# One of four first-layer bias operations moves to GpSimd, and every other group one more to VectorE

## The chip, the cores and the metric

The kernel runs on one core of a Trainium2 chip. A core has TensorE (PE in the profile; PEld is its weight load), VectorE (DVE), ScalarE (ACT), GpSimd (POOL) and SyncE (SP), which work side by side, each through its own instructions in order, and 16 DMA engines. Times are device microseconds (us). The kernel before took 1106.79 us, the median of three runs (1106.64 to 1107.31).

## What is computed

An attention layer with a learned position bias, followed by two gated layers. The part that the change touches is the bias: for every query position and key position a hidden layer of 32 units is made from one number, and a second layer turns it into one bias for each of 8 heads.

```python
scores = scale * np.matmul(q, k.transpose(0, 1, 3, 2))       # 4 batches, 8 heads, 576 positions
psi_rel = np.log1p(np.abs(pos[:, None] - pos[None, :]))
psi_i = np.log1p(np.maximum(pos[:, None], 1.0))
x = (psi_rel / psi_i)[..., None]
h = np.maximum(x @ w1 + b1, 0.0)                              # first layer, 32 hidden units
bias = h @ w2                                                # second layer, 8 heads
scores = scores + bias.transpose(2, 0, 1)[None]
attn = softmax(scores);  x = attn @ v
x = (sigmoid(x @ w_gate) * (x @ w_val)) @ w_out
h = x @ w_in;  out = (h * clip(h + 3, 0, 6) / 6) @ w_out2
```

## The kernel before

The 576 query positions are cut into five chunks: four of 128 and one of 64. For each chunk the kernel makes the bias, then the attention of 32 batch and head pairs (as 16 units of two heads), and then the two gated layers, which are cut into 68 steps. The gated layers of a chunk run together with the bias and the attention of the next chunk in one "block". Only the first chunk's bias and attention stand alone, at the start. That start is called the lead here.

**The bias of a group.** A group is 16 query positions. 32 hidden units times 4 positions fill 128 partitions, so a group takes four first-layer operations, g = 0 to 3, each on 128x576 numbers: `bias_hidden(G, g, act)` at L136. Operations with g below `act` (2, if nothing is said) are done by ScalarE at L147 as relu(x * scale + b1), the others by VectorE at L149 as max(x * scale, -b1). The second form lacks the addition of b1. What is missing is the same for all keys, w2 times b1, and is put back later through the bias column `cv_t` (L120), whose rows 64 to 127 belong to g = 2 and 3. The result of a group is the tile `z`, of 18,432 bytes a partition, from the pool `z_p` of two buffers (L72), which lives for the whole kernel.

TensorE multiplies z with w2, eight products a group (`bias_mm`, L170), each g into its own 32 rows of a PSUM tile. There are two such PSUM tiles. VectorE then writes the group's bias to the tile `bo` (`bias_out`, L227), SyncE copies the first two heads of it to the mask `bm` of the first attention units (L233), and after every second group GpSimd's queue issues the transfer of the pair to `biasD` in memory (L235). For later chunks the bias depends on the distance alone in a simpler way ("mirrored", L162, L195, L201, L190).

**The order.** In the lead the order of the instructions on TensorE, ScalarE, VectorE and SyncE is that of the code (L648). GpSimd's order is left to the planner, which puts the instructions in the order in which it expects them to become ready. Groups 0 to 7 are the first chunk, 8 to 11 the beginning of the second. In the loop at L657 group G's four first-layer operations and products come first, then the output of group G - 1; the output of group 7 comes ahead of group 8. After the loop come the scores of the first unit (`att_qk`, L309), groups 10 and 11 with `act` = 1, and then the loop over the 16 units: exponentials (L334), row factors, transposes (L360) into the tile `pT`, sums with v (`att_av`, L404), and a split of the result into two parts, `xyh` (ScalarE, L424) and `xyl` (VectorE, L425), which the gated layers read.

In the blocks only TensorE and SyncE are in the order of the code; the planner orders VectorE and ScalarE. Groups 12 to 15 belong to the first block, but their z needs nothing of the lead but a free z buffer.

**Memory.** The lead has its own tiles, in pools that are stacked in the order of L646: `pt` (two of 4,608 bytes a partition), `s` (three of 4,608), `k`, `v`, `bo`, `wf`, `cv`. When the lead ends, the pools made by `late` (L705) take the same memory from the beginning on: `bo` first (4,864 bytes), then the tiles of the gated layers. An operation on a late tile waits for the tiles of the lead that lay there.

Of the kernel before, what the change touches and what calls it, by code (L numbers as in the profile page):

```python
# [9 lines left out]
F32 = mybir.dt.float32  # L10
# [9 lines left out]
NI = 288  # L20
# [38 lines left out]
def fused_kernel(ctx: ExitStack, tc: tile.TileContext, qd, kd, vd, tz, td, rd, zc, w2b, iden, wpack, out):  # L59
# [11 lines left out]
    bm_p = pool("bm", 2)  # L71
    z_p = pool("z", 2)  # L72
    w_p = pool("w", 6)
# [20 lines left out]
    zc_t = const.tile([128, 3], F32, name="zc_t")  # L94
    cv_t = const.tile([128, 1], F32, name="cv_t")
    wm_t = const.tile([128, 1], F32, name="wm_t")
    w2b_t = const.tile([128, 32], F32, name="w2b_t")
# [7 lines left out]
    nc.vector.memset(id_t, 0.0)  # L105
    nc.vector.memset(cv_t, 0.0)
    ps = mm_ps()
    for _ in range(9):
# [5 lines left out]
    ps = mm_ps()  # L114
    for g in (2, 3):
        nc.tensor.matmul(
            out=ps[32 * g:32 * g + 32, 0:2], lhsT=w2b_t, rhs=zc_t[:, 0:2], start=True, stop=True,
            tile_position=(0, 32 * g),
        )
    nc.vector.tensor_scalar(out=cv_t[64:128], in0=ps[64:128, 1:2], scalar1=D ** 0.5, scalar2=None, op0=ALU.mult)  # L120

# [14 lines left out]
    def bias_hidden(G, g, act=2):  # L136

        if g == 0:
            z_q[G] = z_p.tile([128, 4, S], F32, name="z")
        t = 4 * G + g  # L140
        if mirrored(G):
            n = reach(G)[2]
            z, x = z_q[G][:, g, 0:n], td_t[:, 0:n]
        else:
            z, x = z_q[G][:, g], tz_t[:, S - 4 - 4 * t:2 * S - 4 - 4 * t]
        if g < act:
            nc.scalar.activation(out=z, in_=x, func=AF.Relu, scale=sc_t[:, t:t + 1], bias=b1c)  # L147
        else:
            nc.vector.tensor_scalar(  # L149
                out=z, in0=x, scalar1=sc_t[:, t:t + 1], scalar2=zc_t[:, 2:3], op0=ALU.mult, op1=ALU.max  # L150
            )
# [25 lines left out]
    def bias_out2(G, apart=False):  # L177
# [6 lines left out]
        if apart:  # L184
            for x, p in enumerate((ps, bo_q.pop(G + 1))):
                nc.scalar.activation(
                    out=bo[:, x, left:SU], in_=p[:, 0:right + 1], func=AF.Identity, scale=D ** 0.5, bias=cv_t
                )
            for x, p in enumerate((ps, p)):
                nc.vector.tensor_scalar(  # L190
                    out=bo[:, x, 0:left], in0=p[:, left:0:-1],
                    scalar1=D ** 0.5, scalar2=cv_t, op0=ALU.mult, op1=ALU.add,
                )
        else:
            nc.scalar.activation(  # L195
                out=bo[:, :, left:SU], in_=ps[:, :, 0:right + 1], func=AF.Identity, scale=D ** 0.5, bias=cv_t
            )
# [18 lines left out]
    def bias_out(G, x=0, last=True):  # L216
# [7 lines left out]
        if c:  # L224
            nc.scalar.activation(out=bv, in_=ps[:, :, 0:NI], func=AF.Identity, scale=D ** 0.5, bias=cv_t)
        else:
            nc.vector.tensor_scalar(  # L227
                out=bv, in0=ps[:, :, 0:NI], scalar1=D ** 0.5, scalar2=cv_t, op0=ALU.mult, op1=ALU.add
            )
# [415 lines left out]
    with ExitStack() as lead:  # L645
        for name, bufs in (("pt", 2), ("s", 3), ("k", 6), ("v", 7), ("bo", 3), ("wf", 2), ("cv", 2)):  # L646
            A[name] = lead.enter_context(tc.tile_pool(name=name + "l", bufs=bufs))
# [9 lines left out]
        for G in range(NG0 + NG1 + 1):  # L657
            if G == NG0:
                bias_out(G - 1, (G - 1) % 2, G % 2 == 0)
            if G < NG0 + NG1:  # L660
                for g in range(4):
                    bias_hidden(G, g)
                bias_mm(G)
# [43 lines left out]

    A["bo"] = late("bo", 1)
    P = dict(gu=late("gu", 12), tmp=late("tmp", 3), acc=late("acc", 4))
    A.update(k=late("k", 4), v=late("v", 4), s=late("s", 2))  # L710
# [213 lines left out]
```

## Time and profile before

| what | value |
|---|---|
| median of three runs | 1106.79 us |
| time of the profiled execution | 1106.79 us |
| its span, first to last instruction | 1105.0 us |
| TensorE busy | 1094.5 us |
| VectorE busy | 668.0 us |
| ScalarE busy | 524.7 us |
| GpSimd busy | 129.7 us |
| first chunk's bias, first z to last output | 4.75 to 20.05 us |
| attention of the first chunk | 24 to 88 us |

In the rows below a time in front is the start in us from the span's start, the second number is how long the instruction or the merged run of instructions lasted; "x2" is their count, and square brackets give the idle time of the engine just before and what ended it. Instructions of one engine can overlap a little: the next begins while the one before drains. A busy TensorE in the rows is not a TensorE at its peak, since matmuls are pipelined and their ends are modelled.

### The profile page before, as it was taken

How to read it: one execution, taken by the hardware profiler on the slowest of the kernel's cores; microseconds unless marked ns; L12 is line 12 of the kernel's file. 1: busy time of each engine (PE TensorE's matmuls, PEld its weight loads, DVE VectorE, ACT ScalarE, POOL GpSimd, SP SyncE). 2: the span in 40 equal slices, each digit the busy share in tenths (PEclk: the TensorE clock that was granted, in tenths of full speed). 3: DMA queues.
4: the chain of work that ended last, by engine and by line, in shares of the span. 5: the costliest groups of instructions: out<-in, count | busy, mean ns of one | idle time of the engine just before them, and what ended most of it. 6: DMA issues, size and time to landing. Idle time of an engine off the chain costs nothing.

```text
span 1105.0 us, 19878 instructions
## 1 busy us (share of the span) xinstructions
PE 1094.5 (99%) x7142; PEld 884.0 (80%) x7142; DVE 668.0 (60%) x1529; ACT 524.7 (47%) x1052; POOL 129.7 (12%) x248
## 2 busy tenths in 40 slices
PE   8999999999999999999999999999999999999998
PEld 4777777777777788777888878788788787879998
DVE  7999998898963456897725654656252417052232
ACT  7887686798863433565414342534032214121132
POOL 1000000000010002112221111111430202031000
PEclk9999999999999999999999999999999999999999
DMA  6958999999987688999988888798896978778997
GB/s 228 369 182 296 373 396 373 386 322 375 384 292 233 219 264 281 283 311 294 342 296 249 292 245 278 250 281 244 283 274 239 266 247 255 227 215 310 363 365 270
DMA packets 118769, 321.97 MB, mean 291 GB/s; under 512 B 21008, under 2 KB 29712, under 8 KB 118672
## 3 DMA queue, kind: packets, MB, share of 16 engines
q1 hardware_dynamic: 108000, 297.15, 79.0%
q0 software_dynamic: 9152, 23.21, 7.5%
q8 instruction: 57, 0.93, 0.3%
q10 hardware_dynamic: 1520, 0.35, 0.1%
q14 instruction: 40, 0.33, 0.1%
HBM read 245.09 MB, written 51.37 MB: 268 GB/s over the span
## 4 chain that ended last, share of the span: by engine, by line
PE 80%; DVE 7%; DMA 5%; ACT 4%; issue 3%; POOL 1%; ACTq 0%; DVEq 0%; POOLq 0%
PE ps L574 63%; PE ps L404 7%; PE ps L309 3%; PE ps L446 3%; PE ps L360 2%; DMA pT<-t 2%; PE ps L162 1%; PE ps L170 1%; DVE cm L546 1%; DMA wsp<-wp 1%; DVE cm L549 1%; DVE wp L555 1%; POOL outT L635 1%; ACT cm L544 1%; DVE s L324 1%
## 5 line engine op out<-in xcount | busy, mean ns | idle before, releaser
L574 PE MATMUL ps<-xyh,wp 128*128 128x512 f32 (+1 forms) x1600 | 468.1, 372 | 0.3
L574 PEld LDWEIGHTS ps<-xyh,wp 128*128 128x128 f32 x1600 | 290.5, 189 | 61.3 <-issue 4.9
L574 PE MATMUL ps<-gh,wp 128*128 128x512 f32 (+1 forms) x1120 | 330.2, 373 | 0.0
L574 PE MATMUL ps<-xyl,wp 128*128 128x512 f32 (+1 forms) x800 | 295.6, 370 | 0.4 <-DVE xyl L587 0.3
L574 PEld LDWEIGHTS ps<-gh,wp 128*128 128x128 f32 x1120 | 203.5, 189 | 37.8 <-issue 3.6
L574 PE MATMUL ps<-gl,wp 128*128 128x512 f32 (+1 forms) x560 | 206.9, 369 | 0.0
L574 PEld LDWEIGHTS ps<-xyl,wp 128*128 128x128 f32 x800 | 151.1, 189 | 24.6 <-DVE xyl L587 0.8
L383 POOL DMA_DIRECT2D pT<-t x192 | 94.3, 499 | 504.1 <-DVE t L373 136.3
L583 ACT ACTIVATE gh<-tmp 128x512 fp32r<-128x512 f32 (+1 forms) x140 | 82.2, 588 | 145.9 <-DVE tmp L605 103.3
L334 ACT ACTIVATE s<-s,m 128x576 f32<-128x576 f32 x144 | 110.4, 768 | 20.1 <-DVE m L468 14.4
L574 PEld LDWEIGHTS ps<-gl,wp 128*128 128x128 f32 x560 | 105.8, 189 | 16.8 <-DVE gl L585 0.6
L585 DVE TENSOR_TENSOR gl<-tmp,gh 128x512 fp32r<-128x512 f32 (+1 forms) x140 | 88.6, 634 | 47.3 <-ACT gh L583 46.4
L605 DVE SCALAR_TENSOR_TENSOR tmp<-tmp,ps 128x512 f32<-128x512 f32 (+1 forms) x60 | 37.8, 630 | 94.1 <-PE ps L574 92.7
L404 PEld LDWEIGHTS ps<-pT,vt 128*64 128x64 f32 x1600 | 79.4, 137 | 18.1 <-issue 12.6
L404 PE MATMUL ps<-pT,vt 128*64 128x128 f32 (+1 forms) x1600 | 92.4, 266 | 1.5 <-DMA pT<-t 0.9
L611 DVE SCALAR_TENSOR_TENSOR tmp<-tmp,ps 128x512 f32<-128x512 f32 (+1 forms) x80 | 50.0, 628 | 57.1 <-ACT tmp L610 55.5
L424 ACT ACTIVATE xyh<-ps 128x128 fp32r<-128x128 f32 (+1 forms) x52 | 16.5, 317 | 107.3 <-PE ps L404 107.1
L610 ACT ACTIVATE tmp<-ps 128x512 f32<-128x512 f32 (+1 forms) x80 | 43.9, 549 | 41.9 <-PE ps L574 40.4
L425 DVE TENSOR_TENSOR xyl<-ps,xyh 128x128 fp32r<-128x128 f32 (+1 forms) x52 | 17.7, 341 | 72.4 <-ACT xyh L424 72.1
L601 ACT ACTIVATE tmp<-ps 128x512 f32<-128x512 f32 (+1 forms) x60 | 33.1, 552 | 56.9 <-PE ps L574 56.9
L635 POOL DMA_DIRECT2D outT<-acc x40 | 27.7, 736 | 262.3 <-DVE acc L626 245.1
L147 ACT ACTIVATE z<-tz_t,zc_t,sc_t 128x576 f32<-128x576 f32 (+7 forms) x70 | 49.7, 766 | 13.2 <-PE ps L162 11.3
(73 smaller groups left out, 1096.5 us busy)
## 6 DMA issues: line engine op xcount, KB each, us to landing
wp<-wsp SPq DMA_DIRECT2D x272, 512.0 KB, 5.2
wd<-wpack SPq DMA_DIRECT2D x68, 512.0 KB, 6.7
wsp<-wp SPq DMA_DIRECT2D x68, 512.0 KB, 6.2
vt<-vd SPq DMA_DIRECT2D x80, 320.0 KB, 5.2
kt<-kd SPq DMA_DIRECT2D x80, 288.0 KB, 5.1
pT<-t POOLq DMA_DIRECT2D x192, 72.0 KB, 5.3
pT<-t SPq DMA_DIRECT2D x128, 72.0 KB, 5.0
bm<-biasD SPq DMA_DIRECT2D x15, 576.0 KB, 5.9
```

Of the source, the lines that this page charges most:

```text
L147: nc.scalar.activation(out=z, in_=x, func=AF.Relu, scale=sc_t[:, t:t + 1], bias=b1c)
L309: nc.tensor.matmul(out=ps[h][n * a:n * a + n, j, 0:NI], lhsT=qt[r, b + a, 0:n], rhs=kt[r, NI * j:NI * j + NI], start=True, stop=True, tile ...
L334: nc.scalar.activation(out=s[:, h], in_=s[:, h], func=AF.Exp, scale=-1.0, bias=d["m"][:, h:h + 1], accum_out=r[:, h:h + 1],)
L383: (nc.sync if p[0][0] < 4 and i > 1 else nc.gpsimd).dma_start(out=pt[32 * q:32 * q + 32, i].rearrange("j u t i -> j (u t i)"), in_=t[32 * ...
L404: nc.tensor.matmul(out=po[64 * h:64 * h + 64, n * a:n * a + n], lhsT=vt[:, v], rhs=pt[:, m * a:m * a + m, k, :], start=(t == 0), stop=(t = ...
L574: nc.tensor.matmul(out=ps[:, 0:nt], lhsT=w[:, c, :], rhs=x[:, 0:nt], start=(first and c == 0 and i == 0), stop=(last and c == 3 and i == 2),)
L583: nc.scalar.activation(out=hi[:, 0:nt], in_=src, func=AF.Copy, scale=scale)
L585: nc.vector.tensor_tensor(out=lo[:, 0:nt], in0=src, in1=hi[:, 0:nt].bitcast(F32), op=ALU.subtract)
L605: nc.vector.scalar_tensor_tensor(out=th, in0=th, scalar=1.0, in1=ps, op0=ALU.add, op1=ALU.mult)
L610: nc.scalar.activation(out=t, in_=ps, func=AF.Relu, bias=3.0)
L611: nc.vector.scalar_tensor_tensor(out=t, in0=t, scalar=6.0, in1=ps, op0=ALU.min, op1=ALU.mult)
L635: q.dma_start(out=out[2 * ih + x, o, :, :, lo - ih * NI:hi - ih * NI], in_=av[:, 2 * x:2 * x + 2, lo - i0:hi - i0],)
```

## The change

Of a first-chunk group's four first-layer operations GpSimd makes the last (g = 3). ScalarE makes the first two in even groups and the first alone in odd ones, and VectorE the rest: one in even groups, two in odd ones. The columns that put w2 times b1 back follow: `cv_t` for groups with two ScalarE operations, the new `cv1_t` for those with one, which is also used for groups 10 and 11. The z tiles come from a pool of three buffers that belongs to the lead, and from a pool of two late buffers after it, which lies behind the late `bo`. The persistent pool is gone.

```diff
-    z_p = pool("z", 2)
...
+    cv1_t = const.tile([128, 1], F32, name="cv1_t")
...
+    nc.vector.memset(cv1_t, 0.0)
...
-    for g in (2, 3):
+    for g in (1, 2, 3):
         nc.tensor.matmul(
             out=ps[32 * g:32 * g + 32, 0:2], lhsT=w2b_t, rhs=zc_t[:, 0:2], start=True, stop=True,
...
-    nc.vector.tensor_scalar(out=cv_t[64:128], in0=ps[64:128, 1:2], scalar1=D ** 0.5, scalar2=None, op0=ALU.mult)
+    for cv, p in ((cv_t, 64), (cv1_t, 64), (cv1_t, 32)):
+        e = max(2 * p, 64)
+        nc.vector.tensor_scalar(out=cv[p:e], in0=ps[p:e, 1:2], scalar1=D ** 0.5, scalar2=None, op0=ALU.mult)
...
-            z_q[G] = z_p.tile([128, 4, S], F32, name="z")
+            z_q[G] = A["z"].tile([128, 4, S], F32, name="z")
...
-            nc.vector.tensor_scalar(
+            (nc.gpsimd if g == 3 and G < NQ // 16 else nc.vector).tensor_scalar(
                 out=z, in0=x, scalar1=sc_t[:, t:t + 1], scalar2=zc_t[:, 2:3], op0=ALU.mult, op1=ALU.max
...
-                out=bv, in0=ps[:, :, 0:NI], scalar1=D ** 0.5, scalar2=cv_t, op0=ALU.mult, op1=ALU.add
+                out=bv, in0=ps[:, :, 0:NI], scalar1=D ** 0.5, scalar2=cv1_t if G % 2 else cv_t,
+                op0=ALU.mult, op1=ALU.add,
...
-        for name, bufs in (("pt", 2), ("s", 3), ("k", 6), ("v", 7), ("bo", 3), ("wf", 2), ("cv", 2)):
+        for name, bufs in (("pt", 2), ("s", 3), ("k", 6), ("v", 7), ("bo", 3), ("z", 3), ("wf", 2), ("cv", 2)):
...
-                    bias_hidden(G, g)
+                    bias_hidden(G, g, 1 if G < NG0 and G % 2 else 2)
...
     A["bo"] = late("bo", 1)
+    A["z"] = late("z", 2)
```

## Rows read from the trace of the kernel before

**Rows 1.** The page, parts 1 and 2: busy time of each engine; granted clock in tenths.

```profile
PE 1094.5 (99%) x7142; PEld 884.0 (80%) x7142; DVE 668.0 (60%) x1529; ACT 524.7 (47%) x1052; POOL 129.7 (12%) x248
...
PEclk9999999999999999999999999999999999999999
```

**Rows 2.** Busy time by stage: stretch, its length, then each engine; clock, DMA share, GB/s.

```profile
0.00:31.00 31.00, 27.12 (x207) 13.09 (x208) 24.68 (x56) 23.80 (x36) 5.57 (x12) 1.00 0.73 242
31.00:82.00 51.00, 50.47 (x525) 39.24 (x525) 46.77 (x142) 42.46 (x115) 0.00 (x0) 1.00 0.75 275
...
89.00:320.00 231.00, 230.51 (x1330) 179.93 (x1330) 211.72 (x438) 182.80 (x358) 3.55 (x6) 1.00 0.99 366
```

**Rows 3.** The chain of waits, 9 to 33 us: start, length, what.

```profile
10.99 8.22 PE ps L170 x78
...
19.96 0.52 DVE z L149
...
24.31 1.24 PE ps L309 x6
```

**Rows 4.** VectorE in order of time, 4.7 to 20.6 us.

```profile
6.83 0.16 DVE L120 TENSOR_SCALAR cv_t<-ps 64x1 f32<-64x1 f32 x1
7.66 0.82 DVE L227 TENSOR_SCALAR bo<-ps,cv_t 128x576 f32<-128x576 f32 x1 [0.66 <-PE ps L170]
...
11.81 1.06 DVE L149 TENSOR_SCALAR z<-tz_t,sc_t,zc_t 128x576 f32<-128x576 f32 x2
12.78 0.81 DVE L227 TENSOR_SCALAR bo<-ps,cv_t 128x576 f32<-128x576 f32 x1
13.51 1.06 DVE L149 TENSOR_SCALAR z<-tz_t,sc_t,zc_t 128x576 f32<-128x576 f32 x2
...
16.92 1.06 DVE L149 TENSOR_SCALAR z<-tz_t,sc_t,zc_t 128x576 f32<-128x576 f32 x2
...
19.23 0.82 DVE L227 TENSOR_SCALAR bo<-ps,cv_t 128x576 f32<-128x576 f32 x1 [0.53 <-PE ps L170]
```

**Rows 5.** ScalarE in order of time, 4.7 to 20.6 us.

```profile
4.75 14.23 ACT L147 ACTIVATE z<-tz_t,zc_t,sc_t 128x576 f32<-128x576 f32 x18 [1.09 <-DVE sc_t L112]
```

**Rows 6.** TensorE's weight loads in order of time, 4.7 to 12 and 19 to 25 us.

```profile
6.43 0.90 PEld L170 LDWEIGHTS ps<-z,w2b_t 128*32 128x32 f32 x16 [0.62 <-ACT z L147]
...
20.52 0.14 PEld L162 LDWEIGHTS ps<-z,w2b_t 128*32 128x32 f32 x2 [1.35 <-DVE z L149]
...
24.30 0.78 PEld L309 LDWEIGHTS ps<-kt,qt 64*128 64x128 f32 x6 [1.29 <-ACT bo L201]
```

**Rows 7.** SyncE's queue of transfers in order of time, 8 to 22 us.

```profile
8.51 12.69 SPq L233 DMA_DIRECT2D bm<-bo  x16
```

**Rows 8.** GpSimd in order of time, 4.7 to 20.6 us.

```profile
13.89 0.82 POOL L235 DMA_DIRECT2D biasD<-bo  x1 [2.53 <-DVE bo L227]
```

**Rows 9.** Groups by line and shape, 4 to 24 us: busy us, mean ns of one.

```profile
L147 ACT ACTIVATE z<-tz_t,zc_t,sc_t 128x576 f32<-128x576 f32 x16 | 12.6, 857 | 1.3 <-DVE sc_t L112 1.1
L149 DVE TENSOR_SCALAR z<-tz_t,sc_t,zc_t 128x576 f32<-128x576 f32 x16 | 8.4, 571 | 0.0
L227 DVE TENSOR_SCALAR bo<-ps,cv_t 128x576 f32<-128x576 f32 x8 | 6.5, 811 | 1.2 <-PE ps L170 1.2
```

**Rows 10.** VectorE in order of time, 26 to 29 us.

```profile
26.60 0.87 DVE L149 TENSOR_SCALAR z<-tz_t,sc_t,zc_t 128x384 f32<-128x384 f32 x2
```

**Rows 11.** ScalarE in order of time, 82 to 89 us.

```profile
85.25 2.51 ACT L147 ACTIVATE z<-tz_t,zc_t,sc_t 128x384 f32<-128x384 f32 x4
87.65 0.27 ACT L424 ACTIVATE xyh<-ps 128x128 fp32r<-128x128 f32 x1
```

**Rows 12.** TensorE's weight loads in order of time, 82 to 89 us.

```profile
85.62 0.63 PEld L404 LDWEIGHTS ps<-pT,vt 128*64 128x64 f32 x10 [0.37 <-ACT cm L544]
...
87.97 0.19 PEld L574 LDWEIGHTS ps<-xyh,wp 128*128 128x128 f32 x1 [0.56 <-ACT xyh L424]
88.48 0.18 PEld L574 LDWEIGHTS ps<-xyl,wp 128*128 128x128 f32 x1 [0.33 <-DVE xyl L425]
```

More of the change, by code (lines that the diff above doesn't have):

```diff
@@ L186, in bias_out2 @@
                 nc.scalar.activation(
-                    out=bo[:, x, left:SU], in_=p[:, 0:right + 1], func=AF.Identity, scale=D ** 0.5, bias=cv_t
+                    out=bo[:, x, left:SU], in_=p[:, 0:right + 1], func=AF.Identity, scale=D ** 0.5, bias=cv1_t
                 )
@@ L191, in bias_out2 @@
                     out=bo[:, x, 0:left], in0=p[:, left:0:-1],
-                    scalar1=D ** 0.5, scalar2=cv_t, op0=ALU.mult, op1=ALU.add,
+                    scalar1=D ** 0.5, scalar2=cv1_t, op0=ALU.mult, op1=ALU.add,
                 )
```

## The prediction, made before the changed kernel was run

> **What bounds the kernel now.** I read the busy shares first. TensorE is busy for 1094.5 of 1105.0 us and the clock that it was granted stands at its upper level of 2.4 GHz in every slice [rows 1]. The table by stages says where the other 10 us are: from 31 us on TensorE is busy in nearly every microsecond, and before that it is busy for 27.12 of 31.00 us [rows 2]. What starts the attention earlier therefore ends the kernel earlier, as long as nothing later has its own clock. The profiled execution took 1106.79 us around a span of 1105.0 us, so 1.79 us lie outside the span; it is also the median of the three runs, and I add gains and losses straight onto 1106.79.
>
> Then the chain of waits of the front: TensorE's L170 (first-chunk bias products) up to 19.2 us, then VectorE's z, ScalarE's bias output, and from 24.31 us on TensorE with scores, transposes and sums [rows 3]. That chain names TensorE for 10.99 to 19.21 us, but it only merges a queue that is filled in time; the row of VectorE shows the real pace. Between the first output (7.66) and the last (19.23) no idle time stands before any of its rows: two z, one bias output, two z. Two z begin at 11.81, the output at 12.78, the next z at 13.51 [rows 4]. So one z is worth (12.78 - 11.81) / 2 = 0.485 us of VectorE, the output 0.73 us, a group 1.70 us. ScalarE is nearly as full: 18 operations in 14.23 us [rows 5], 0.79 us each, 1.58 a group. TensorE waits for ScalarE in the first groups (0.62 us at 6.43, and as long again in each of the two groups behind it) [rows 6]. SyncE's sixteen copies of the output to the first mask take 12.69 us in all with their waits, 1.59 a group [rows 7]; they come behind the output and do not set its pace. GpSimd only issues one DMA for every two groups, 0.8 us each, and sleeps 2.5 us between them [rows 8].
>
> The end of the stage is the last bias output, at 19.23 us; VectorE had waited 0.53 us for TensorE there. Its last z before ended at 16.92 + 1.06 = 17.98 us, so from a group's last z to its output TensorE needs 1.25 us [rows 4]. Everything after hangs on that output: z of group 8 at 19.96, TensorE's group 8 at 20.52 after 1.35 us of waiting, ScalarE's output, the second half of the first scores at 24.30 after 1.29 us [rows 3, 6].
>
> **The change part by part.** *ScalarE* makes 12 instead of 16 z in the stage: 1.5 x 0.79 = 1.19 us a group. It is off the path.
>
> *VectorE* makes 1 z in even groups, 2 in odd ones. Bias output to bias output: 0.73 + 0.485 = 1.215 us or 1.70 us. Start: the first output stands at 7.66 us, 0.66 us after VectorE was free [rows 4], for TensorE waits for ScalarE's second z there [rows 6]; that stays. From it six steps, three of 1.215 and three of 1.70, are 8.75 us; TensorE's 1.25 us against a step of 1.215 adds about 0.05 three times, 0.15. So the seventh output starts at 16.56, the last z ends about 0.08 later (one operation begins as the last drains), and the eighth output starts at 16.64 + 1.25 = 17.89 instead of 19.23: a gain of 1.34 us, if GpSimd is in time and in nobody's way.
>
> *GpSimd* makes one z a group, on 128x576. No row shows GpSimd computing on such a tile; its memory fills are one column wide. Bounds: below, VectorE's 571 ns; above, 1.62 us, twice the bias output's 811 ns (two steps a column). I take 0.81 us: the output's row has the same 576 columns at one a step, and ScalarE's 857 ns says the same [rows 9]. With its half DMA a group (0.41) that is 1.22 us a group, under the 1.46 of VectorE.
>
> *Does GpSimd's work stop VectorE's?* VectorE's z takes 571 ns where its output takes 811 ns for the same columns [rows 9]; in pace 0.485 against 0.73. So z runs at about two columns a step. No row shows a GpSimd computation beside it. The DMA issue at 13.89 [rows 8] lies beside the z pair at 13.51, which takes 1.06 us like the pair at 11.81 [rows 4]; but an issue does not stream a tile. The ends are: nothing, or the two operations wholly one after the other. The second costs, by the walk: at the start VectorE's three z go first (4.75 + 3 x 0.485 = 6.21), GpSimd's first z then ends at 7.02 where TensorE would have wanted it from 6.43: 0.6 us. Later GpSimd's buffer comes free when TensorE ends a group, just as VectorE starts an output; 0.73 us of GpSimd's 0.81 are then covered and 0.08 is not. GpSimd starts about 0.30 us after what it waits for (output 12.78 + 0.81 = 13.59, issue 13.89) [rows 4, 8], so up to 0.38 is not. For five such groups that is 0.4 to 1.9 us; I take 0.8, since the lag is free wherever GpSimd waits for a z to end anyway. Together 1.4 us, which eats the gain: 1.34 - 1.4 = -0.06. I take this end, for an operation at double rate leaves least for a second reader; that is an inference, not a row.
>
> The Trainium skill, page "SBUF — State Buffer", section "Who interferes with whom", says that VectorE in a two-port mode and GpSimd hold one shared port pair in turn, each for a whole instruction. By that rule the time is the one with the 1.4 us, without it the one with none; the issue at 13.89 shows no such stop and no run here has yet shown a tile operation.
>
> *Third buffer.* Before, a group's first z waits until TensorE has ended the group two back; now three back. This lets GpSimd and ScalarE run ahead; it is in the walk above.
>
> *Constants.* One more tiny product, two more 0.16 us columns and a memory fill. VectorE was idle for 0.66 us before 7.66 and does one z less before it [rows 4]: nothing. Without that cover 0.3 us.
>
> *The z buffers after the stage.* They now lie in memory that the stage's own tiles used: 4,864 bytes in, so the first covers the last unit's transposed scores and two score tiles. VectorE's two z of group 12, made at 26.60 us [rows 10], can no longer be made there; they come after the last unit's sum, whose last operands are in at 85.62 + 0.63 = 86.25 [rows 12]. ScalarE's z of group 12 too, and that helps: at 85.25 four z of 2.51 us lie ahead of the last xyh at 87.65, and TensorE idles 0.56 us for it and 0.33 us for the xyl behind it [rows 11, 12]. At best 0.89 us come back; at worst VectorE's extra 0.87 us delay a weight's split and cost as much. In the stage 89 to 320 us VectorE is 92% busy but TensorE waits little [rows 2]. I take a gain of 0.3 us.
>
> **Sum, forecast:** 1106.79 + 0.06 - 0.3 = 1106.55, say 1106.5 us. Alone, with the ends of its terms: 1.34 - 1.0 + 0.89 better is 1105.6, 2.5 - 1.34 + 0.87 worse is 1108.8.
>
> **The rivals.** *No exclusion.* The whole 1.34 us are kept: 1106.79 - 1.34 - 0.3 = 1105.2 us (1104.6 to 1106.3 with the last term's ends). For it: the unmoved z beside the issue. Against: an issue is no tile operation.
>
> *GpSimd is slow (slower side).* With exclusion, time beyond 0.81 us is not covered by the 0.73 us output, and about seven of the eight operations pass it on: 0.1 us more of GpSimd is 0.7 us more of kernel. At 1.2 us it is 1106.5 + 2.7 = 1109.2; at 1.62 us, 1112.2. It decides for "slower" from 0.81 + 2.5 / 7 = 1.17 us on. For it: GpSimd has no fast row anywhere. Against: 1.17 us is 1.4 times the output's row for the same columns.
>
> The Trainium skill, page "GPSIMD Engine Reference", section "Key points", has elementwise work structurally about twice as fast on VectorE. Twice 571 ns would be 1.14 us and the time 1106.5 + 0.33 x 7 = 1108.8 us.
>
> *GpSimd's own queue.* Its order is left to the planner. If the pair's DMA stands ahead of the z of group 3, 5 and 7, each odd group waits for: output 0.81, start 0.30, issue 0.82, z 0.81, TensorE 1.25 = 4.0 us for two groups against 3.4 now. From the second output (about 8.9) three such rounds end at 20.9, 1.7 us late: 1106.79 + 1.7 - 0.3 = 1108.2 us. Against: z of group 3 is ready some 2 us before that DMA. This is also how the change would not do what it says.
>
> **How the numbers follow.** Chances: forecast 0.45, no exclusion 0.26, slow GpSimd 0.17, queue 0.12. I predict 1106.5 us. The range 1104.8 to 1109.4 leaves out the far end of "no exclusion" and the upper half of "slow GpSimd", some 0.16. A measurement of this kernel can tell about 0.2%, 2.2 us, from no change, so same is 1104.6 to 1109.0. Faster: the far end of "no exclusion", 0.07. Slower: most of "slow GpSimd" and a bit of the queue, 0.17. Same: 0.76.
>
> **What the changed profile would show.** A GpSimd z of 0.7 to 0.9 us; VectorE z stretched or held next to it; outputs 1.5 to 1.8 us apart on average; the last at 18.9 to 19.6 us; scores' second half near 24.3 us. "No exclusion": VectorE's z all at 0.57 us and the last output near 17.9. "Slow": a GpSimd row over 1.17 us and TensorE waiting for POOL. "Queue": the DMA ahead of the odd z on POOL. The third part: no z at 26.6 us, and xyh of the last unit right behind its sum. Wrong altogether would be a shift at 31 us that is not found at the end: then something later, the weight stream of 89 to 320 us, has a clock of its own.

## The result, and the profile after

The changed kernel took 1120.35 us, the median of five runs (1117.71 to 1122.77), against 1106.84 us of the kernel before in the same session; the ratio is 1.011 with a 95% interval of 1.0089 to 1.0131. That is 1.1% slower, clear of the noise, and far outside the predicted 1104.8 to 1109.4 us. The profiled execution of the changed kernel took 1117.85 us around a span of 1115.8 us, with TensorE granted its upper level of 2.4 GHz in every slice as before [rows 1]; everything below explains that execution. Three of the five runs were 2.5 to 5 us longer at a mean granted clock of 0.995 to 0.998; no profile of this kernel shows such a run, so where in it the clock was lower stays open.

Where the time went can be read off TensorE's rows by looking up the same instruction in both traces. "No. 200" is the product of the gated layers (L574 before, L578 after) that stands 200 behind the first one of its block.

| instruction of TensorE | before, us | after, us | later by |
|---|---|---|---|
| last bias output (VectorE) | 19.23 | 27.14 | 7.91 |
| first transpose of the attention | 30.94 | 38.87 | 7.93 |
| first product of the gated layers | 84.50 | 92.93 | 8.43 |
| no. 200 of the first block | 136.36 | 146.74 | 10.37 |
| no. 400 of the first block | 199.54 | 211.78 | 12.24 |
| first product of the fourth block | 796.38 | 808.68 | 12.30 |
| no. 200 of the fourth block | 847.95 | 859.07 | 11.12 |
| last instruction | 1105.01 | 1115.82 | 10.81 |

So there are two losses: 7.9 us before the attention starts, and 3.8 us in the first block between 93 and 212 us. Half a us more goes between 39 and 93 us, and 1.5 us come back late (1.2 of it in the fourth block, at a wait described under the reasons). The rest of 1117.85 - 1106.79 = 11.06 us lies outside the span.

**The front.** The groups by line and shape, 4 to 28 us of the changed kernel (busy us, mean ns of one, idle time before and who ended it); they answer rows 9:

```profile
L152 POOL TENSOR_SCALAR z<-tz_t,sc_t,zc_t 128x576 f32<-128x576 f32 x8 | 19.4, 2433 | 4.4 <-DVE sc_t L113 4.3
...
L150 ACT ACTIVATE z<-tz_t,zc_t,sc_t 128x576 f32<-128x576 f32 x12 | 9.8, 860 | 5.9 <-PE ps L173 3.0 <-DVE z L152 1.7 <-DVE sc_t L113 1.1
L152 DVE TENSOR_SCALAR z<-tz_t,sc_t,zc_t 128x576 f32<-128x576 f32 x12 | 9.0, 783 | 0.0
L230 DVE TENSOR_SCALAR bo<-ps,cv_t 128x576 f32<-128x576 f32 x8 | 6.5, 818 | 7.9 <-PE ps L173 7.9
```

GpSimd's z takes 2433 ns, three times what I took. VectorE, which had no idle time in this stage but 1.2 us [rows 9], now idles 7.9 us before its outputs. GpSimd in order of time, which answers rows 8:

```profile
4.80 12.23 POOL L152 TENSOR_SCALAR z<-tz_t,sc_t,zc_t 128x576 f32<-128x576 f32 x5 [4.35 <-DVE sc_t L113]
16.98 0.91 POOL L239 DMA_DIRECT2D biasD<-bo  x1
17.93 4.84 POOL L152 TENSOR_SCALAR z<-tz_t,sc_t,zc_t 128x576 f32<-128x576 f32 x2
22.72 0.76 POOL L239 DMA_DIRECT2D biasD<-bo  x1
23.54 2.35 POOL L152 TENSOR_SCALAR z<-tz_t,sc_t,zc_t 128x576 f32<-128x576 f32 x1
```

It works without a gap from 4.80 us to 23.54 + 2.35 = 25.89 us: eight z and two DMA issues in between. TensorE's 1.25 us from a last z to its output [rows 4] put the eighth output at 27.14 us, and there it stands (the profile calls GpSimd's spans rough; that this sum fits speaks for these). TensorE's weight loads, which answer rows 6, show the same from the other side (three of the eight that wait for POOL), and below them the sum of all such waits from 0 to 39 us:

```profile
9.70 0.64 PEld L173 LDWEIGHTS ps<-z,w2b_t 128*32 128x32 f32 x16 [1.63 <-POOL z L152]
12.17 0.64 PEld L173 LDWEIGHTS ps<-z,w2b_t 128*32 128x32 f32 x14 [1.82 <-POOL z L152]
...
20.55 0.64 PEld L173 LDWEIGHTS ps<-z,w2b_t 128*32 128x32 f32 x16 [2.02 <-POOL z L152]
```

```profile
PEld ps L173 <- POOL z L152: 12.8, 8, 2.0
```

VectorE, which answers rows 4, is stretched next to GpSimd, but never held for a whole GpSimd operation (a pair of z took 1.06 us before):

```profile
10.90 0.82 DVE L230 TENSOR_SCALAR bo<-ps,cv_t 128x576 f32<-128x576 f32 x1 [0.93 <-PE ps L173]
11.63 1.78 DVE L152 TENSOR_SCALAR z<-tz_t,sc_t,zc_t 128x576 f32<-128x576 f32 x2
13.37 0.82 DVE L230 TENSOR_SCALAR bo<-ps,cv_t 128x576 f32<-128x576 f32 x1
14.10 0.79 DVE L152 TENSOR_SCALAR z<-tz_t,sc_t,zc_t 128x576 f32<-128x576 f32 x1
```

**The first block.** ScalarE, VectorE and TensorE's weight loads of the changed kernel around the end of the lead; they answer rows 10 to 12:

```profile
94.97 0.28 ACT L428 ACTIVATE xyh<-ps 128x128 fp32r<-128x128 f32 x1 [1.16 <-PE ps L408]
95.14 2.50 ACT L150 ACTIVATE z<-tz_t,zc_t,sc_t 128x384 f32<-128x384 f32 x4
97.53 0.62 ACT L558 ACTIVATE wp<-cm 128x512 fp32r<-128x512 f32 x1
```

```profile
95.27 1.65 DVE L152 TENSOR_SCALAR z<-tz_t,sc_t,zc_t 128x384 f32<-128x384 f32 x4
96.83 0.69 DVE L550 SCALAR_TENSOR_TENSOR cm<-wd,cm 128x512 uint32<-128x512 uint32 x1
97.43 0.29 DVE L429 TENSOR_TENSOR xyl<-ps,xyh 128x128 fp32r<-128x128 f32 x1
```

```profile
97.77 0.19 PEld L578 LDWEIGHTS ps<-xyl,wp 128*128 128x128 f32 x1 [1.69 <-DVE xyl L429]
```

The last xyh now comes right behind its sum, ahead of ScalarE's z. But VectorE's z, all four of groups 12 and 13, and a weight step now stand ahead of xyl, and TensorE waits 1.69 us for it, where it waited 0.56 + 0.33 us in all [rows 12]. Before, VectorE made the two of group 12 at 26.60 us [rows 10] and the two of group 13 here, ahead of the last unit but one:

```profile
82.54 0.86 DVE L149 TENSOR_SCALAR z<-tz_t,sc_t,zc_t 128x384 f32<-128x384 f32 x2
```

After that TensorE waits for weights; here are its waits for the two engines that make them, 90 to 215 us (us in total, times, longest). Before, the first of these was 1.0 us in two waits, and the second did not occur:

```profile
PEld ps L578 <- DVE wp L559: 3.4, 6, 1.0
...
PEld ps L578 <- ACT wp L558: 1.5, 2, 0.8
```

### The profile page after: what moved, and what is told of

The parts are those of the page before. It is cut to its first block, busy times and chain, and to the rows that moved or that the text cites. A ratio compares the mean times of both kernels' runs of the same rounds, so it can differ in the third digit from the quotient of the medians.

```text
span 1115.8 us, 19898 instructions
## 1 busy us (share of the span) xinstructions
PE 1093.9 (98%) x7144; PEld 882.1 (79%) x7144; DVE 669.5 (60%) x1528; ACT 522.4 (47%) x1048; POOL 149.5 (13%) x256
## 4 chain that ended last, share of the span: by engine, by line
PE 90%; DVE 4%; DMA 2%; issue 1%; ACT 1%; POOL 1%; SPq 0%; DVEq 0%; ACTq 0%; POOLq 0%
PE ps L578 72%; PE ps L408 7%; PE ps L313 3%; PE ps L364 3%; PE ps L450 2%; PE ps L165 2%; POOL z L152 1%; PE ps L456 1%; DMA wd<-wpack 1%; DVE s L328 0%; DVE cm L550 0%; PE ps L173 0%; ACT z L150 0%; DMA wp<-wsp 0%; DVE s L351 0%
## 5 line engine op out<-in xcount | busy, mean ns | idle before, releaser
L578 PE MATMUL ps<-xyh,wp 128*128 128x512 f32 (+1 forms) x1600 | 467.7, 372 | 1.8 <-DVE wp L559 1.0
L578 PEld LDWEIGHTS ps<-xyh,wp 128*128 128x128 f32 x1600 | 289.9, 189 | 63.8 <-issue 5.4
L578 PE MATMUL ps<-gh,wp 128*128 128x512 f32 (+1 forms) x1120 | 330.1, 372 | 0.0
L578 PE MATMUL ps<-xyl,wp 128*128 128x512 f32 (+1 forms) x800 | 295.4, 369 | 1.6 <-DVE xyl L429 1.3
L578 PEld LDWEIGHTS ps<-gh,wp 128*128 128x128 f32 x1120 | 203.4, 189 | 37.9 <-issue 3.6
L578 PE MATMUL ps<-gl,wp 128*128 128x512 f32 (+1 forms) x560 | 206.6, 369 | 0.5 <-DVE gl L589 0.5
L578 PEld LDWEIGHTS ps<-xyl,wp 128*128 128x128 f32 x800 | 150.9, 189 | 26.2 <-DVE xyl L429 1.7
L578 PEld LDWEIGHTS ps<-gl,wp 128*128 128x128 f32 x560 | 105.7, 189 | 17.4 <-DVE gl L589 1.3
L377 DVE STREAM_TRANSPOSE t<-s 128x1152 f32<-128x1152 f32 x40 | 54.3, 1370 | 4.3 <-DMA vt<-vd 2.0
```

The costliest lines, as they stand in the source:

```text
L377: nc.vector.transpose(out=tn_q[0][:, :, x], in_=st[u]["s"].rearrange("p h j -> p (h j)").rearrange("p (t q j) -> p q t j", q=4, j=32),)
L578: nc.tensor.matmul(out=ps[:, 0:nt], lhsT=w[:, c, :], rhs=x[:, 0:nt], start=(first and c == 0 and i == 0), stop=(last and c == 3 and i == 2),)
```

## The experiments

Eleven runs; the second one of the odd groups stands in the text alone. "Later by" is always against the profile of the kernel before; where a kernel was only run once, it is this, not the time, that the reading rests on. The kernel before had medians of 1106.84 to 1107.61 us beside them.

| kernel | first transpose | first gated product | no. 400, first block | last instruction | time, us |
|---|---|---|---|---|---|
| after | +7.93 | +8.43 | +12.24 | +10.81 | 1120.35 |
| e1, no GpSimd | +1.61 | +1.96 | +5.83 | +3.78 | 1111.62 |
| e2, z pools alone | -0.02 | +0.16 | +4.76 | +3.64 | 1110.01 |
| e3, late z elsewhere | +7.99 | +8.56 | +8.53 | +6.94 | 1114.61 |
| e4, no z on VectorE | +6.85 | +7.32 | +12.09 | +9.82 | 1116.79 |
| e5, prices | +0.36 | +0.48 | +1.18 | +0.37 | 1107.16 |
| e6, half the columns | +1.00 | +0.99 | +0.94 | -0.32 | 1106.66 |
| e7, three buffers | +0.08 | +1.08 | +1.26 | +1.54 | 1107.67 |
| e8, odd groups | -0.19 | +1.56 | +1.77 | +0.63 | 1106.77 |
| e9, ScalarE's z behind | +0.13 | +0.14 | +6.47 | +5.80 | 1112.69 |
| e10, beside | +0.54 | +0.54 | +1.93 | +0.98 | 1107.77 |

**Without GpSimd.**

```diff
-            (nc.gpsimd if g == 3 and G < NQ // 16 else nc.vector).tensor_scalar(
+            nc.vector.tensor_scalar(
```

> The changed kernel with GpSimd's operation given back to VectorE: VectorE makes two of a group's four in even groups and three in odd ones, and everything else of the change (the three buffers, the late z pool, the second column) stays. Theory: the 7.9 us by which the first transposes come late (38.87 against 30.94 us) are GpSimd's pace. Then VectorE sets it: a step is 0.73 + 0.97 = 1.70 us or 0.73 + 1.455 = 2.185 us; six steps from 7.66 are 11.66, the last output at 7.66 + 11.66 + 0.08 + 1.25 = 20.65 instead of 19.23, first transposes at about 32.4 us. The loss behind 31 us (+0.5 at the first gated step, +3.8 more in the first block) stays, for it comes from the late z: end near 1106.8 + 1.4 + 2.5 = 1110.7 us (1109.5 to 1112). Rival: the loss behind the front is a consequence of the late start of the front itself: then it goes too, end near 1108.2 us.

Measured: 1111.62 us, median of five, ratio 1.0041 (1.0028 to 1.0055); the profiled execution took 1110.6 us. Of the 7.93 us at the first transpose 6.32 are GpSimd's. What is left, 1.61 us, is VectorE's third z in odd groups: its outputs stand at 9.52 and 11.71 us, 2.19 us apart, which is 0.73 + 3 x 0.485. The loss in the first block is there without GpSimd and its late front (5.83 - 1.96 = 3.87 us), so the rival fell.

**The z pools alone.** The kernel before, with the pools of the change and nothing else of it.

```diff
-    z_p = pool("z", 2)
...
-            z_q[G] = z_p.tile([128, 4, S], F32, name="z")
+            z_q[G] = A["z"].tile([128, 4, S], F32, name="z")
...
+        (..., ("bo", 3), ("z", 3), ("wf", 2), ("cv", 2)):
...
     A["bo"] = late("bo", 1)
+    A["z"] = late("z", 2)
```

> The kernel before with only the z pools of the change: three buffers in the lead, two late ones behind the late output tile; all engines as before. Theory: the third buffer gives the front at most 0.3 us (last output 18.9 to 19.2 us); VectorE's two z of group 12 leave 26.6 us, all four z of groups 12 and 13 stand ahead of the last xyl, TensorE waits 1.3 to 1.7 us there, and VectorE's backlog of weights costs 1 to 2.5 us more between 97 and 165 us: end 1108.5 to 1110.5 us. Rival (the late z costs nothing by itself, the loss needs the late front): 1106.5 to 1107 us.

Measured: 1110.01 us, median of ten, ratio 1.0024 (1.0014 to 1.0033). The front does not move (-0.02 us), so the third buffer gives nothing by itself. The first block loses 4.6 us, with the same two marks as in the changed kernel: the wait for xyl below, and the waits for weights behind it. The rival, no loss without a late front, fell.

```profile
89.49 0.19 PEld L573 LDWEIGHTS ps<-xyl,wp 128*128 128x128 f32 x1 [1.68 <-DVE xyl L424]
```

**The late z in another place.** The changed kernel, with the late z buffers where the lead's own z buffers lay, behind the tiles of the gated layers. (One z tile, 4 x 576 numbers of 4 bytes, has 9,216 bytes a partition; the 18,432 given at the start are two of them.)

```diff
     A["bo"] = late("bo", 1)
-    A["z"] = late("z", 2)
     P = dict(gu=late("gu", 12), tmp=late("tmp", 3), acc=late("acc", 4))
+    A["z"] = late("z", 2)
```

> The changed kernel with the late z pool moved behind the gated layers' accumulators, where the lead's own z tiles and third output tile lay, which are free at about 33 us. Theory: VectorE's z of groups 12 and 13 are made ahead of the lead's end again (in the thirties and at the last units), no four z ahead of the last xyl; the front stays 7.9 us late. The loss behind it (2.9 us in the profiled execution of the changed kernel) goes for the most part: end 1114.5 to 1115.5 us. Rival (the loss behind the front has another cause): as the changed kernel, 1117.7 us or more.

Measured: 1114.61 us, median of four, ratio 1.0073 (1.0054 to 1.0092). The first block no longer loses anything: +8.56 us at its first product, +8.53 at the 400th. Its ScalarE rows have the order of the kernel before again, z ahead of the last xyh, and TensorE has its two short waits back:

```profile
93.82 2.49 ACT L150 ACTIVATE z<-tz_t,zc_t,sc_t 128x384 f32<-128x384 f32 x4
96.22 0.25 ACT L428 ACTIVATE xyh<-ps 128x128 fp32r<-128x128 f32 x1
```

```profile
96.52 0.19 PEld L578 LDWEIGHTS ps<-xyh,wp 128*128 128x128 f32 x1 [0.54 <-ACT xyh L428]
97.04 0.19 PEld L578 LDWEIGHTS ps<-xyl,wp 128*128 128x128 f32 x1 [0.34 <-DVE xyl L429]
```

**Three buffers with the late ones in that place.** The same move in the kernel of the pools alone, so the kernel before with other z buffers.

```diff
-    A["z"] = late("z", 2)
     P = dict(gu=late("gu", 12), tmp=late("tmp", 3), acc=late("acc", 4))
+    A["z"] = late("z", 2)
```

> The kernel before with the z buffers of the change alone (three in the lead, two late ones), but the two late ones lie behind the tiles of the gated layers' accumulators, where the lead's own z tiles were, and not behind the late bias output. Theory (what cost 3.6 us with the buffers alone was the place, over tiles that the last unit of the lead still uses): no loss behind the front, the first transpose within 0.3 us of before, the block's wait chain as before, time 1105.6 to 1107.3. Rival (any z tiles that end with the lead bring the planner's order of the first block out of step): again 2 us or more lost between 85 and 200 us, time from 1109 us on.

Measured: 1107.67 us, median of ten, ratio 0.9989 (0.997 to 1.0009), not to be told from before. The median lies 0.4 us above the range that I gave; in the profiled run TensorE's weight loads once stood 1.00 us up to 40.53 us, and 0.8 us of the wait of the products there ended with the transfer of the keys. In the first block 0.2 us are lost instead of 4.6. Both pairs (after and e3, e2 and e7) differ in the place alone: it is the place that cost. The four kernels with the first place (after, e1, e2, e4) lose 3.8 to 4.8 us in the first block, the four with the other one (e3, e6, e7, e8) at most 0.2.

**GpSimd's price.** The kernel before, with eight GpSimd operations of several forms between 50 and 65 us, into a tile that nobody reads.

```diff
...
+        for n in (S, S, S // 2, S // 4):
+            nc.gpsimd.tensor_scalar(
+                out=pr_t[:, 0:n], in0=x[:, 0:n], scalar1=p, scalar2=zc_t[:, 2:3], op0=ALU.mult, op1=ALU.max
+            )
+        nc.gpsimd.tensor_scalar(out=pr_t, in0=x, scalar1=p, scalar2=None, op0=ALU.mult)
+        nc.gpsimd.tensor_scalar(out=pr_t, in0=x, scalar1=1.5, scalar2=0.25, op0=ALU.mult, op1=ALU.max)
+        nc.gpsimd.tensor_scalar(out=pr_t, in0=x, scalar1=1.5, scalar2=None, op0=ALU.mult)
+        nc.gpsimd.tensor_copy(out=pr_t, in_=x)
...
```

> The kernel before, and on GpSimd, idle otherwise, a row of extra operations beside the attention of the first chunk, whose results nobody reads: the operation of the change on 576 columns twice, on 288 and on 144, then on 576 with one arithmetic step, with numbers instead of columns as operands (two steps, one step), and a copy. Theory (GpSimd's own price): 2.2 to 2.4 us for 576 columns here too, where VectorE's z do not run; 1.2 and 0.65 us for 288 and 144. Rival (VectorE's z at double rate stretch it): 0.6 to 1.0 us here, against 2.27 to 2.58 us in the changed kernel. The forms tell what in the operation costs: if the column operands do, the forms with numbers are well shorter; if the second step does, the one-step forms are. Time: no change, 1106.8 us, or 0.3 us more.

Measured: the groups by line and shape of GpSimd, 48 to 70 us:

```profile
L131 POOL TENSOR_SCALAR pr_t<-tz_t,r,zc_t 128x576 f32<-128x576 f32 x2 | 5.3, 2662 | 20.8 <-ACT pT L375 20.7
L135 POOL TENSOR_SCALAR pr_t<-tz_t 128x576 f32<-128x576 f32 x1 | 2.4, 2393 | 0.1
L134 POOL TENSOR_SCALAR pr_t<-tz_t,r 128x576 f32<-128x576 f32 x1 | 1.8, 1799 | 0.1
L136 POOL TENSOR_SCALAR pr_t<-tz_t 128x576 f32<-128x576 f32 x1 | 1.7, 1710 | 0.1
L131 POOL TENSOR_SCALAR pr_t<-tz_t,r,zc_t 128x288 f32<-128x288 f32 x1 | 1.4, 1377 | 0.1
L131 POOL TENSOR_SCALAR pr_t<-tz_t,r,zc_t 128x144 f32<-128x144 f32 x1 | 1.0, 1047 | 0.1
L137 POOL COPY pr_t<-tz_t 128x576 f32<-128x576 f32 x1 | 0.7, 662 | 0.1
```

The form of the z costs 2.66 us here. The theory had 2.2 to 2.4 us, 1.2 for 288 columns and 0.65 for 144; all three came out longer, and the rival's 0.6 to 1.0 us fell. VectorE works on the attention beside these operations, and each of the other forms ran once, so differences of a few tenths say nothing. Dropping one of its two arithmetic steps takes it to 1.80 us, dropping both (a copy) to 0.66 us; whether its operands are columns or plain numbers matters little (2.39 and 1.71 us). A quarter of the columns still costs 1.05 us, so a large part of the time does not go with the columns.

**No z on VectorE.** The changed kernel, but in the first chunk ScalarE makes three z of a group, GpSimd one, VectorE none (the bias column follows).

```diff
...
-                    bias_hidden(G, g, 1 if G < NG0 and G % 2 else 2)
+                    bias_hidden(G, g, 3 if G < NG0 else 2)
```

> The changed kernel, but in the first chunk ScalarE makes three of a group's four z, GpSimd the fourth and VectorE none; everything else, the late z buffers too, as in the changed kernel. Theory (GpSimd's own price): its z still takes 2.3 to 2.5 us with no VectorE z beside it, eight of them with the DMA issues between them still set the stage's pace (ScalarE's three z are 3 x 0.79 = 2.4 us a group, just under it), and the first transpose stands within 1 us of the changed kernel's +7.93 us against before; time 1116.5 to 1119. Rival (VectorE's two-per-step z hold GpSimd up): its z falls to 1.8 us or less, the pace is then ScalarE's 2.4 us a group, and since that is what GpSimd needs today too, the first transpose alone would not tell; the duration of the GpSimd row does.

Measured: 1116.79 us in one run, and GpSimd's group, 4 to 28 us:

```profile
L154 POOL TENSOR_SCALAR z<-tz_t,sc_t,zc_t 128x576 f32<-128x576 f32 x8 | 18.2, 2278 | 4.6 <-DVE sc_t L115 4.5
```

2278 ns is the price with nothing of VectorE's next to it but its outputs, 2433 ns the price next to VectorE's z: of GpSimd's time 0.16 us is company, the rest its own. The rival's 1.8 us or less did not come. The first transpose moved by 6.85 us, 1.08 us less than in the changed kernel and so just outside the 1 us that I gave.

**Beside, but not in the way.** The kernel before; four operations of the z's form run on GpSimd in the first stage, and nobody waits for their result.

```diff
...
+        for t in range(4):
+            nc.gpsimd.tensor_scalar(
+                out=pr_t, in0=tz_t[:, S - 4 - 4 * t:2 * S - 4 - 4 * t],
+                scalar1=sc_t[:, t:t + 1], scalar2=zc_t[:, 2:3], op0=ALU.mult, op1=ALU.max
+            )
```

> The kernel before, and in its first stage GpSimd makes four operations of the form of the z on the first chunk's data, into a tile that nobody reads; no engine waits for them but GpSimd's own DMA issues behind them. So only what GpSimd takes from the others by working beside them is left. Theory (partial sharing): GpSimd's operations take 2.3 to 2.6 us, VectorE's z next to them are stretched by 0.2 to 0.45 us for each GpSimd operation, as in the changed kernel (0.79 and 1.07 us where the trace of before has 0.57), and the first transpose moves by 0.3 to 1.5 us. Rival 1 (one of the two stands still for the whole of the other's instruction): VectorE loses some 2.3 us for each, the first transpose moves by 5 us or more. Rival 2 (they do not touch each other, the stretched z waited for something else): VectorE's z stay at 0.57 us and the first transpose within 0.3 us.

Measured: 1107.77 us in one run. GpSimd and VectorE, 4 to 20 us, by groups:

```profile
L659 POOL TENSOR_SCALAR pr_t<-tz_t,sc_t,zc_t 128x576 f32<-128x576 f32 x4 | 9.8, 2444 | 4.6 <-DVE sc_t L112 4.4
L149 DVE TENSOR_SCALAR z<-tz_t,sc_t,zc_t 128x576 f32<-128x576 f32 x16 | 9.2, 618 | 0.0
```

VectorE's sixteen z take 618 instead of 571 ns [rows 9]: 16 x 0.047 = 0.75 us for four GpSimd operations, 0.19 us each. The first transpose moved by 0.54 us. That is partial sharing. Both rivals fall: one that stands still for the other would have cost 2.3 us each, and no touch at all would have left 571 ns. The clearest rows are these; the second of the two GpSimd operations runs from 7.92 to 10.20 us, and the two z of VectorE that lie wholly inside it take 1.06 us, as before:

```profile
4.90 5.30 POOL L659 TENSOR_SCALAR pr_t<-tz_t,sc_t,zc_t 128x576 f32<-128x576 f32 x2 [4.45 <-DVE sc_t L112]
```

```profile
8.57 1.06 DVE L149 TENSOR_SCALAR z<-tz_t,sc_t,zc_t 128x576 f32<-128x576 f32 x2
```

This kernel also lost 1.4 us in the first block, with no z moved; I have no cause for that, and take it as a measure of what in that block can't be put down to an edit.

**Half the columns.** Three buffers with the late ones in the harmless place; in every group GpSimd makes 288 of the 576 columns of g = 3 and VectorE the others, and ScalarE its two.

```diff
...
+            parts = ((nc.gpsimd, 0, NI), (nc.vector, NI, S)) if g == 3 and G < NQ // 16 else ((nc.vector, 0, z.shape[1]),)
+            for e, j0, j1 in parts:
+                e.tensor_scalar(
+                    out=z[:, j0:j1], in0=x[:, j0:j1],
...
```

> The kernel with three early z buffers and the late ones behind the accumulators, and in it GpSimd makes the first 288 of the 576 columns of the fourth z in every group, VectorE the other 288; the shares of ScalarE stay. Theory (GpSimd's time goes with its columns, 1.38 us for 288, and with the issues it is 1.8 us a group against the 1.65 us of the stage): eight operations of 1.4 to 1.6 us and three issues of 0.8 us from 4.9 us on end at 18.5 to 20.1 us where TensorE wants the last one at about 17.4 us, so the first transpose is 0.5 to 2.5 us late and the time 1107 to 1109.5 us. Rival (what costs is the handing over between two engines of one tile, not the columns): as late as in the changed kernel, 5 us or more.

Measured: the first transpose 1.00 us late, inside 0.5 to 2.5; GpSimd's last z ends at 17.45 + 1.51 = 18.96 us, inside 18.5 to 20.1. The single time, 1106.66 us, is below the range that I gave, since 1.2 us came back at the wait in the fourth block. Handing one tile to two engines costs nothing that shows; the columns do.

**GpSimd in odd groups alone.** The same buffers; GpSimd makes g = 3 of groups 1, 3, 5 and 7, where VectorE made it. It was timed in two sessions.

```diff
-            nc.vector.tensor_scalar(
+            (nc.gpsimd if g == 3 and G < NQ // 16 and G % 2 else nc.vector).tensor_scalar(
```

> The kernel with three early z buffers and the late ones behind the accumulators, and in it GpSimd makes one z in groups 1, 3, 5 and 7 alone, where VectorE made it; the shares of ScalarE stay. Theory (GpSimd's 2.4 us a z is what cost the time, and it has 3.4 us for two groups): z of group 1 runs 4.8 to 7.2, of 3 to about 10.0, a DMA issue, of 5 to 13.2, a DMA issue, of 7 to 16.4; each ends before TensorE asks for it, VectorE saves four times 0.485 us, but ScalarE's 16 z of 0.79 us each then end the stage, so the last bias output gains 0 to 0.7 us; time 1105 to 1107. Rival (VectorE is held for the length of each GpSimd operation): four times 2.4 us are taken from VectorE, the last output is 3 us or more late, time from 1109 us on.

> The kernel with GpSimd in groups 1, 3, 5 and 7 alone, the same as before, timed again in more rounds on another chip or at another time, beside the kernel before. Theory (the front is 0.2 us earlier, and the first loads of keys that come 1 to 2 us later then decide): 0.0 to 0.8 us below the kernel before, ratio 0.9993 to 1.0000, not to be told from it. Rival (a real gain): ratio 0.998 again, its interval below 1.

Measured: 1106.77 us, median of ten, ratio 0.998 (0.9963 to 0.9997), and the second time 1108.08 us, median of twelve, ratio 1.0004 (0.999 to 1.0017). GpSimd in order of time shows slack (0.38 us before its second z, 0.43 us before an issue), and TensorE never waits for it:

```profile
4.96 2.58 POOL L148 TENSOR_SCALAR z<-tz_t,sc_t,zc_t 128x576 f32<-128x576 f32 x1 [4.50 <-DVE sc_t L111]
7.92 2.28 POOL L148 TENSOR_SCALAR z<-tz_t,sc_t,zc_t 128x576 f32<-128x576 f32 x1 [0.38 <-PE ps L169]
10.63 0.91 POOL L234 DMA_DIRECT2D biasD<-bo  x1 [0.43 <-DVE bo L226]
11.58 2.61 POOL L148 TENSOR_SCALAR z<-tz_t,sc_t,zc_t 128x576 f32<-128x576 f32 x1
```

At this share GpSimd costs nothing, and the last output stands at 19.02 instead of 19.23 us. What VectorE saves, four times 0.485 us, is mostly lost again: its twelve z take 688 instead of 571 ns, 1.4 us in all, and TensorE still waits 3.7 us for ScalarE's z (4.0 us before; 4 to 24 us). The 0.2 to 0.3 us at the first transpose did not become a gain of the kernel: in the first profile TensorE's weight loads stood 1.89 us up to 37.46 us, and the view of the keys' tile puts 1.7 us of that, on its products, down to the transfer of the keys, which came no earlier. The interval of the first session lies just below 1, that of the second holds 1, so a real gain is not shown. No version found beats the kernel before.

**ScalarE's late z held back.** The kernel before with one tie more.

```diff
+    last_xh = issued[1]
...
+            def hid(G=G0 + g):
+                with ExitStack() as behind:
+                    if c == 1:
+                        behind.enter_context(tc.issue_after(last_xh.ins))
+                    for t in range(4):
+                        bias_hidden(G, t)
```

> The kernel before with one tie more: ScalarE's z of groups 12 to 15 stand behind the split (xyh) of the lead's last unit. Theory (the four z at 85.25 us, 2.51 us, hold xyh up, and TensorE waits 0.56 us for it and 0.33 us for xyl): both waits go, block 0 starts up to 0.9 us earlier, time 1105.9 to 1106.6 if nothing later has its own pace. Rival (the weight stream of the first block has its own pace on VectorE and ScalarE, so an earlier start ends in a wait there): the gain at the first gated product is gone by its 200th, time 1106.7 or more; the z that were moved then stand in the way of ScalarE's share of the weights and can cost up to 2.5 us.

Measured: 1112.69 us, median of ten, ratio 1.0048 (1.0027 to 1.0068). My theory, a gain of up to 0.9 us, fell. The wait for xyh is gone, but VectorE's two z of group 13, which the planner moved along from 82.54 to 86.97 us, stand ahead of xyl (0.91 us of waiting), and the weights fall behind: +0.14 us at the first product, +2.91 at no. 200, +6.47 at no. 400. Up to no. 200 that is the loss of the z pools alone (2.77 us in both), though group 12's two z stayed at 26.73 us here. Behind no. 200 a part of it is TensorE's clock. In this execution alone of those in the table it fell to the lower level of 1.2 GHz within the work, from 145.7 to 149.1 us, after TensorE had waited twice for weights; its products then took 0.63 instead of 0.40 us (stretch, length, busy time of PE, PEld, DVE, ACT, POOL, clock, DMA share, GB/s):

```profile
144.40 0.50 PE L574 MATMUL ps<-xyh,wp 128*128 128x512 f32 x1 [1.34 <-ACT wp L554]
144.74 0.40 PE L574 MATMUL ps<-xyl,wp 128*128 128x512 f32 x1
146.14 1.22 PE L574 MATMUL ps<-xyh,wp 128*128 128x512 f32 x2 [1.01 <-DVE wp L555]
147.16 0.63 PE L574 MATMUL ps<-xyl,wp 128*128 128x512 f32 x1
```

```profile
145.70:149.10 3.40, 2.96 (x7) 2.38 (x8) 3.37 (x7) 2.35 (x4) 0.00 (x0) 0.50 0.98 365
```

TensorE was busy for 2.96 us of it, so the clock's part is some 1.5 us, an estimate. The rival had the direction; its size, up to 2.5 us, was too small even without the clock: the shortest run, 1111.58 us, had a mean granted clock of 1.000. Since both engines' z moved, this run does not tell which of the two costs more.

## Why the prediction was wrong

**What held.** TensorE's stage up to 31 us bounds the kernel: 7.93 us at the first transpose are 8.43 us at the first gated product. VectorE's pace of 0.485 us a z and 0.73 us an output held (2.19 us for three and one without GpSimd). ScalarE's relief was worth nothing (it idled 5.9 us in the stage), the constants cost nothing (they lie in VectorE's wait for TensorE), the third buffer gave nothing by itself (-0.02 us). The marks set for "slow GpSimd" are the ones that came: a GpSimd row over 1.17 us and TensorE waiting for POOL.

**The step that failed first: GpSimd's z at 0.81 us.** It is the term that carried the sum, and its upper bound, 1.62 us, was twice VectorE's output. It measured 2.28 us alone and 2.43 us in company; no factor on another engine's row had a reason to be an upper bound. Each arithmetic step costs GpSimd some 0.7 to 1.1 us on this tile (2.66, 1.80 and 0.66 us with two, one and none), while VectorE's pair with two steps takes 1.06 us and its pair with one step 0.95 us (z, and the scaling of the scores, L347 of before). With the right price the walk is short: eight z and two issues fill GpSimd from 4.80 to 25.89 us, and 1.25 us later the last output stands where it was measured. At 2.43 us a z the price per 0.1 us that I gave for "slow GpSimd" would make about 1117.8 us, close to 1117.85, but by accident: the front gave 7.9 us of the loss and the first block 3.8.

**GpSimd's queue.** Its DMA issues did come between the z (at 16.98 and 22.72 us), as that rival had it, for 0.8 to 0.9 us each, but behind five z and not ahead of the third. On an engine that was already the bound they added 1.7 us.

**The exclusion, 1.4 us.** The Trainium skill, page "SBUF — State Buffer", section "Who interferes with whom", has one of the two hold the shared ports for a whole instruction while the other is blocked. The runs speak against it for this form: next to GpSimd operations of 2.3 to 2.6 us a VectorE z grew by 0.19 us each in e10, by (783 - 571) x 12 / 8 = 0.32 us each in the changed kernel, and GpSimd's by 0.16 us; the longest z of VectorE took 1.07 us. The measurement decides: a toll, not a lock. That VectorE's z ran in a two-port mode is inferred from its pace alone. That VectorE's outputs, which read PSUM, stayed at 0.81 to 0.82 us agrees with the same section, by which a VectorE instruction with at most one input from SBUF, outside the two-port modes, is not touched. When the toll falls and when not (in e10 it was 0.43, 0, 0.23 and 0.11 us by operation) is open.

**The step that failed second: the late z, taken as a gain of 0.3 us between 0.89 either way.** It cost 3.8 us in the changed kernel, 4.6 alone, and its sign was wrong. I priced one wait, xyh behind ScalarE's z. That wait did go. But I had group 12's two z of VectorE coming late, where it was all four, and they and a weight step stood ahead of xyl. Nor did I price what comes behind: ScalarE's 2.50 us, which had stood ahead of the last xyh, and VectorE's 1.65 us now fall behind it, when both split weights for the first block, VectorE being 92% busy there [rows 2]. The supply starts late and TensorE waits for weights up to 163.9 us. "TensorE waits little" in that stage was, as I read it now, true of a supply with a head start, not of a supply with slack. That the place costs is shown; how the late start is handed on is read from the waits, and no run isolates it. Nor is the split the only link: TensorE's chain of waits runs through a transfer of weights too, 6.65 us from 133.44 us on, as it did before (6.71 us from 121.27 us on).

**What came back.** In the kernel before, TensorE stands still once in the fourth block, in this row of its weight loads:

```profile
830.47 0.66 PEld L404 LDWEIGHTS ps<-pT,vt 128*64 128x64 f32 x19 [1.05 <-issue]
```

The changed kernel and the ten others of the table do not have it there; each gets some 1.2 us back. The kernel of the odd groups, profiled twice, lacks it the first time and waits 1.8 us there the second time, so it goes with the execution and not with an edit. What it waits for is open. It is why a front that is 1 us late (e6) can end 0.3 us early: on this kernel a single time says less than 1 us.

## What to carry to other kernels

Price an operation on an engine by a row of that engine, in that form; where the trace has none, the range is open at the top, and the question to ask is at which price the verdict turns (1.17 us in the prediction) and how sure one is to stay under it. Work given to a slow engine costs nothing only as far as that engine is free in the pace of the stage: one z for two groups fitted, without a gain; one for each did not. Memory that is shared between stages is an order: a tile laid over one that is read last can only be written last, so lay early work of the next stage over what comes free early.

## What the runs showed of the hardware that was not expected

- GpSimd on 128x576 numbers of 32 bits: 2.28 us alone for multiply and maximum, 1.71 to 1.80 us for the multiply alone, 0.66 us for a copy; 1.38 us for 288 columns and 1.05 us for 144 with both steps (all but the first beside the attention's work on VectorE, one operation each). VectorE takes 0.57 us for the first of these.
- That is 4.0 times, where the Trainium skill, page "GPSIMD Engine Reference", section "Key points", has elementwise work about twice as fast on VectorE. Its section "Engine selection" has operations with one input at roughly line rate; of the rows here the copy (0.66 us) comes near VectorE's 0.57 us, the arithmetic does not.
- A GpSimd operation and VectorE's z, side by side, slow each other by 0.16 to 0.35 us for each GpSimd operation, in the mean; no z of VectorE waited for a GpSimd operation to end (1.07 us at most, against 2.3 us and more).
- TensorE's granted clock fell to 1.2 GHz for 3.4 us in the execution in which it had waited longest for weights in the first block (e9, waits of 1.34 and 1.01 us).
